# Cross attention and a leaky-ReLU layer on one core: tokens loaded a batch earlier, a gate ahead of their casts, another order in batches 3 to 6

## Chip, core and metric

The kernel runs on one core of one Trainium2 chip. The metric is the device time of one execution in microseconds. Three runs of the kernel before took 202.87 to 203.16 us, with a median of 203.11.

## What is computed

There are 8 batches. Each has 8 heads with 512 tokens and 32 state rows of 64 numbers. Tokens read the state and the state reads the tokens, both with a softmax. The results are laid side by side (544 rows of 512 numbers a batch) and go through a two-layer network.

```python
scores = scale * np.matmul(x, state.transpose(0, 1, 3, 2))
a = softmax(scores)                     # minus the maximum, exp, over (sum + 1e-9)
xread = np.matmul(a, state)
scores2 = scale * np.matmul(state, x.transpose(0, 1, 3, 2))
a2 = softmax(scores2)
sread = np.matmul(a2, x)
attn = np.concatenate([xread, sread], axis=2)
...
h = x @ w_in                            # x: attn as (8 * 544, 512); w_in 512 x 2048
g = np.maximum(0.01 * h, h)
return (g @ w_out).astype(np.float32)   # w_out 2048 x 512
```

## The kernel before

The token rows of a batch go through the first layer without `xread` being formed: the state is multiplied by `w_in` once per batch (the tile `M`, in four column blocks `c`), and `h` is the product of the probabilities `aT` with `M`. The second layer of a batch is a Strassen-like scheme: seven products `n` = 1 to 7 of eight steps each, with sums of halves of `hT` (`su0` to `su3`) and sums of the weights (`tw_...`). One step is a *unit*: two matmuls of 256 columns. A quarter of the first layer (`FastQuad`) is done with seven products too, with sums `lq`.

The work is software-pipelined over batches. While batch `b` has its first layer, batch `b - 1` finishes its second layer, batch `b + 1` has its scores and softmax, and the tokens of batch `b + 2` are loaded (one fp32 buffer `xl`), cast to bf16 by GpSimd (`xb`) and transposed by DMA (`xT`).

Every engine works through its own instructions in the order in which the code issues them; semaphores tie the engines together. SyncE (SP) issues the DMAs of that list in order too. In batches 3 to 6 the order is a string, `ORDER`, which `stretch` goes through token by token. Batches 0 to 2 and 7 are written out. Only the order within each engine counts. The tokens:

- `u`: the next unit, of the batch before while it has any, then of this batch (15 of 56 are done in a batch's own stretch). `d.n`, `dn.n`: what follows product `n`: a copy out of PSUM (1, 6, 5, 7) or a join with a saved copy into the output tile (2, 3, 4), and behind 3 and 4 the output's DMA. `sb.n.m`, `sn.n.m`: four steps (m to m+3) of the sum `su n`, for the batch before or this one.
- `f.j`, `r.j`: block `j` of the first layer (two matmuls of 512 columns into a PSUM tile `ph`, of which there are two) and its leaky ReLU on ScalarE, L411.
- `qs.i`, `g.n`, `gt.n`, `gl`, `gr`: the quad's sums `lq` (L635, two instructions each), products (two matmuls of 256 columns, tile `pl`, L651), evictions and joins (L663 on ScalarE or VectorE, join L666), the GpSimd addition and the ReLUs.
- `S`, `tp`, `rw`, `ls`, `x2`, `ex`, `e2`, `rc`, `ml`, `p2`: the next batch's scores (tile `sc`), first maxima (`mrow`, L226), their transpose (`mrowb`, L234), the subtraction (`sh`, L239), second maxima, exponentials, sums and reciprocals, products, second reciprocals.
- `mk.c`, `ev.c.g`: block `c` of `M` on TensorE and its eviction, whole (`g` = 2) or by halves, on ScalarE (`A`) or VectorE (`V`). A `3` belongs to this batch, the others to the next.
- `loads`, `casts.h`, `turn`: the load of tokens, the cast of two heads, the DMA transpose `xT`. `a2t`: the DMA transpose of the second probabilities. `rows`: in odd batches the state's reads of two batches (`psn`, 64 small matmuls) and their scaling `sr_n`. `rows_t`: their DMA transpose in batch 4. `late.i`: a sum of weights in batch `i`.

Some tiles share buffers by a tag. The quad's saved copies lie where `mrowb` (`gt.1`) and `sh` (`gt.5`) were, and its sums `lq` share two buffers with `xT`.

Of the kernel before, what the change touches and what calls it, by code (L numbers as in the profile page):

```python
# [9 lines left out]
P = 128  # L10
B, H, S, D = 8, 8, 512, 64
NS = 32
DFF = 2048
DM = 512
# [9 lines left out]
FP32 = mybir.dt.float32  # L24
# [6 lines left out]
def kernel(  # L31
# [9 lines left out]
    nc = tc.nc  # L41

    consts = ctx.enter_context(tc.tile_pool(name="consts", bufs=1))
# [61 lines left out]
    def load_x(b, eng):  # L105
        xl[b] = xpool.tile([P, H, NT * D], FP32, name="xl", tag="xl", bufs=1)
        eng.dma_start(xl[b][:], x[b].rearrange("h (p t) d -> p h (t d)", t=NT))

    def open_xb(b):
        xs[b] = xpool.tile([P, NT, H, D], BF16, name="xb", tag="xb")  # L110
# [88 lines left out]
    def a_xt_dma(a):  # L199
        nc.sync.dma_start_transpose(  # L200
            a.xT[:].rearrange("p t k q -> p (t k) q"),
            a.xb[:].rearrange("p t h d -> p (t h d)"),
        )
# [223 lines left out]
    class FastIn:  # L427
# [62 lines left out]
        def done(self, r, n, bank):  # L490
            R = self.R
            if n == 1:
                pool, tag, bufs, n4 = ((xpool, "xb", 4, 2), (mpool, "M", 2, 4))[r]
                ts = [pool.tile([P, n4, R * P], FP32, name=f"sf{r}", tag=tag, bufs=bufs) for _ in range(4 // n4)]
                self.sv[r] = dict(zip((1, 6, 5, 7), [t[:, i] for t in ts for i in range(n4)]))
            sv = self.sv[r]
            flat = bank.rearrange("p q t -> p (q t)")

            def relu(i, c, src):
                nc.scalar.activation(  # L500
                    out=self.hT[:, 8 * i + R * r:8 * i + R * (r + 1), P * c:P * (c + 1)],
                    in_=src.rearrange("p (q t) -> p q t", q=R), func=AF.Prelu, alpha=0.01,
                )

            if n in (1, 6, 7):
                SCA(sv[n], flat)
            elif n == 5:
                VEC(sv[n], flat)
            if n in (2, 3):
                k = {2: 1, 3: 6}[n]  # L510
                nc.vector.tensor_tensor(out=sv[k], in0=flat, in1=sv[k], op=ALU.add)
                relu(0, n - 2, sv[k])
            elif n == 7:
                nc.gpsimd.tensor_tensor(out=sv[5], in0=sv[7], in1=sv[5], op=ALU.add)
            elif n == 4:
                relu(1, 1, sv[5])
                relu(1, 0, flat)
# [192 lines left out]
    HC = DM // 2  # L710
# [68 lines left out]
    class Batch:  # L779
# [44 lines left out]
        def done(self, n, bank, copy=SCA):  # L824
            f = self.f
            if n in (1, 6, 5, 7):
                f.save(n, bank, copy)
            if n == 2:
                f.join(self.yo(0)[:, :, :HC], bank, 1)
                if self.b == B - 1:  # L830
                    self.out(0, slice(0, HC))
            elif n == 7:
                nc.gpsimd.tensor_tensor(  # L833
                    out=self.yo(1)[:, :, HC:], in0=f.sv[7][:], in1=f.sv[5][:], op=ALU.add
                )
                if self.b == B - 1:
                    self.out(1, slice(HC, DM))
            elif n == 3:
                f.join(self.yo(0)[:, :, HC:], bank, 6)
                self.out(0, slice(HC if self.b == B - 1 else 0, DM))  # L840
            elif n == 4:
                f.join(self.yo(1)[:, :, :HC], bank, 7)
                self.out(1)
# [355 lines left out]
        before.f.sums(n, 0, 4)  # L1199
    a_a2t(a1)  # L1200

    def stretch(b, hT, before, now, order):
        a, nxt = att_of[b], att_of[b + 1]
        rel, pm = {}, {}

        def u():
            (before if before.units else now).run(1, quiet=True)

        def f(j):
            rel[j] = ff1(a, hT, j, later=True)

        def mk(c, tag):
            pm[c] = a_m(a if c == 3 else nxt, c, tag)

        def ev(c, g, copy):
            t, src = (a if c == 3 else nxt), pm[c]
            if g == 2:
                copy(t.M[:, :, DM * c:DM * (c + 1)], src[:])  # L1220
            else:
                copy(t.M[:, g, DM * c:DM * (c + 1)], src[g][:] if isinstance(src, list) else src[:, g, :])

        def rows():
            if b % 2:
                a_sread_rows([att_of[b - 2], att_of[b - 1]])

        def loads():
            if b + 2 < B:
                load_x(b + 2, nc.sync)  # L1230

        def casts(h):
            if b + 2 < B:
                if h == 0:
                    open_xb(b + 2)
                cast_x(b + 2, h, h + 2, POO)

        def turn():
            if b + 2 < B:
                a_open(att_of[b + 2], b + 2)  # L1240
                a_xt_dma(att_of[b + 2])

        def rows_t():
            if b == 4:
                sread_t(0, 3)

        def late(i):
            if b == i:
                fi.w_sum(2 * (b - (B - 3)))

        def qs(i):
            if i == 0:
                fq_of[b] = FastQuad(a, 8)
                fq_of[b].hT = hT
            fq_of[b].sums(i)

        table = dict(
            u=u, f=f, r=lambda j: rel.pop(j)(), S=lambda: a_scores(nxt), mk=mk, ev=ev, rows=rows, loads=loads,
            casts=casts, turn=turn, late=late, rows_t=rows_t,
            tp=lambda: a_top(nxt), rw=lambda: a_rows(nxt), ls=lambda: a_less(nxt), x2=lambda: a_max2(nxt),  # L1260
            ex=lambda: a_exp(nxt), e2=lambda g: a_exp2(nxt, g), rc=lambda: a_probs(nxt, 0), ml=lambda: a_probs(nxt, 1),
            p2=lambda: a_probs2(nxt), a2t=lambda: a_a2t(a),
            sb=lambda n, m, k=4: before.f.sums(n, m, m + k), sn=lambda n, m: now.f.sums(n, m, m + 4),
            d=lambda n, copy=SCA: before.done(n, before.bank[n], copy), dn=lambda n, copy=SCA: now.done(n, now.bank[n], copy),
            g=lambda n: fq_of[b].product(n), gt=lambda n, copy=None: fq_of[b].take(n, copy),
            gl=lambda: fq_of[b].last(), gr=lambda i, c: fq_of[b].relu(i, c), qs=qs,
        )
        for name in order.split():
            name, *args = name.split(".")
            table[name](*(int(v) if v.isdigit() else {"A": SCA, "V": VEC}.get(v, v) for v in args))  # L1270

    fi = FastIn(None)
    fq_of = {}
    ORDER = (
# [8 lines left out]
    )  # L1283

    for b in range(2, B):
        hT = hpool.tile([P, 16, S], BF16, name="hT", tag="hT")
        a = att_of[b]
        nxt = att_of[b + 1] if b + 1 < B else None
# [17 lines left out]
        for s in range(16):  # L1306
# [68 lines left out]
            if s == (9 if b == 2 else 7) and b + 2 < B:  # L1375
                a_open(att_of[b + 2], b + 2)
                a_xt_dma(att_of[b + 2])
            if nxt is not None:
                if b == 2 and s < ms:
                    if s in (8, 9):  # L1380
                        a_exp2(nxt, s - 8)
                    elif s == 7:
                        a_exp(nxt)
                        weights_sum(3, 0, 4)
                        a_probs(nxt, 0)
                elif s == 5:
                    a_exp(nxt)
                elif s in (7, 8):
                    a_exp2(nxt, s - 7)
                    if s == 7:  # L1390
                        a_probs(nxt)
                elif s == ms + 1:
                    for some in ((a1, a2, nxt) if b == 2 else (nxt,)):
                        a_probs2(some)
                elif s in (ms + 2, ms + 3):
                    SCA(nxt.M[:, s - ms - 2, DM:2 * DM], pm1[:, s - ms - 2, :])
# [36 lines left out]
    u, v = [psum.tile([P, 1, HC], FP32, name="yu", tag="ph")[:] for _ in range(2)]  # L1433
# [65 lines left out]
```

## Time and profile before

| | |
|---|---|
| median of three runs | 203.11 us (202.87 to 203.16) |
| profiled execution | 202.62 us, of which the span from the first to the last instruction is 200.8 |
| TensorE (PE) busy | 193.4 us, 96% of the span |
| VectorE (DVE) busy | 169.1 us, 84% |
| ScalarE (ACT) busy | 148.3 us, 74% |
| GpSimd (POOL) busy | 61.5 us, 31% |
| moved by DMA | 28.02 MB, mean 139 GB/s |

Times in the views are microseconds from the span's start. A line of the timeline gives start, duration, engine, line of the code, operation, output and inputs, shapes and a count; in brackets stands the idle time ahead of it and what ended it. A matmul's duration includes its way through the array, so matmuls that follow each other without a gap overlap: their starts tell the pace. A group's line gives count, busy time and the mean duration in nanoseconds. Some matmul records are missing in the trace (three in each of these batches).

### The profile page before, as it was taken

How to read it: one execution, taken by the hardware profiler on the slowest of the kernel's cores; microseconds unless marked ns; L12 is line 12 of the kernel's file. 1: busy time of each engine (PE TensorE's matmuls, PEld its weight loads, DVE VectorE, ACT ScalarE, POOL GpSimd, SP SyncE). 2: the span in 40 equal slices, each digit the busy share in tenths (PEclk: the TensorE clock that was granted, in tenths of full speed). 3: DMA queues.
4: the chain of work that ended last, by engine and by line, in shares of the span. 5: the costliest groups of instructions: out<-in, count | busy, mean ns of one | idle time of the engine just before them, and what ended most of it. 6: DMA issues, size and time to landing. Idle time of an engine off the chain costs nothing.

```text
span 200.8 us, 5078 instructions
## 1 busy us (share of the span) xinstructions
PE 193.4 (96%) x2068; PEld 137.1 (68%) x2090; DVE 169.1 (84%) x285; ACT 148.3 (74%) x275; POOL 61.5 (31%) x86
## 2 busy tenths in 40 slices
PE   7999999999999999899999999999999999999992
PEld 2666634346676766776776677677767788799882
DVE  2576689998999999998999799999999977995622
ACT  3378848499877858797899778987898768767710
POOL 8392175790047004220413040400040024004250
PEclk9999999999999999999999999999999999999999
DMA  6999997999661960539162935161006502210035
GB/s 199 215 206 266 236 295 139 226 277 203 139 193 30 302 210 9 108 141 268 64 124 102 265 111 106 69 172 25 3 37 207 99 0 90 122 55 0 5 91 170
DMA packets 39511, 28.02 MB, mean 139 GB/s; under 512 B 25344, under 2 KB 36736, under 8 KB 39488
## 3 DMA queue, kind: packets, MB, share of 16 engines
q1 hardware_dynamic: 33712, 20.35, 38.6%
q0 software_dynamic: 4944, 6.55, 16.1%
q10 hardware_dynamic: 832, 0.79, 1.2%
q8 instruction: 16, 0.26, 0.5%
q14 instruction: 7, 0.06, 0.1%
HBM read 17.30 MB, written 8.91 MB: 131 GB/s over the span
## 4 chain that ended last, share of the span: by engine, by line
PE 76%; DVE 16%; ACT 2%; DMA 2%; issue 2%; DVEq 0%
PE yq L761 32%; PE ph L405 12%; PE py L690 4%; PE pyw L690 3%; PE pf L483 3%; PE yu L761 3%; PE ph L1040 3%; PE pm L384 3%; DVE su L750 3%; DVE lq L635 2%; PE pspin L142 2%; PE pl L651 2%; DMA a2T<-e 2%; PE pl L572 2%; DVE yo L773 2%
## 5 line engine op out<-in xcount | busy, mean ns | idle before, releaser
L411 ACT ACTIVATE hT<-ph 128x512 bf16<-128x512 f32 x84 | 49.0, 605 | 13.3 <-PE ph L405 6.6
L761 PEld LDWEIGHTS <-su 128*128 128x128 bf16 x480 | 45.9, 98 | 13.8 <-issue 0.8
L405 PE MATMUL ph<-aT,M 128*128 128x512 bf16 x148 | 43.5, 379 | 0.4
L761 PEld LDWEIGHTS <-hT 128*128 128x128 bf16 x336 | 32.3, 98 | 12.6 <-issue 2.5
L761 PE MATMUL yq<-tw_xf,su 128*128 128x256 bf16 x224 | 32.8, 273 | 0.2
L761 PE MATMUL yq<-w_out_bf,hT 128*128 128x256 bf16 x224 | 30.3, 273 | 0.3
L113 POOL CAST xb<-xl 128x512 bf16<-128x512 f32 (+1 forms) x24 | 13.6, 608 | 47.5 <-DMA xl<-in_x_dram 36.9
L833 POOL TENSOR_TENSOR yo<-sv,sv 128x512 f32<-128x512 f32 x7 | 9.1, 1298 | 37.5 <-ACT hT L411 28.1
L405 PEld LDWEIGHTS <-M 128*128 128x128 bf16 x168 | 16.4, 98 | 6.2 <-DVE tw_x L727 0.2
L750 DVE TENSOR_TENSOR su<-hT 128x1024 bf16<-128x1024 bf16 (+1 forms) x27 | 18.8, 702 | 0.8 <-ACT hT L411 0.6
L770 ACT COPY sv<-yq 128x512 f32<-128x512 f32 x24 | 13.9, 585 | 5.5 <-PE yq L761 5.4
L761 PE MATMUL yq<-tw_x,su 128*128 128x256 bf16 x112 | 16.1, 273 | 0.0
L761 PE MATMUL yq<-w_out_bf,su 128*128 128x256 bf16 x112 | 16.0, 273 | 0.1
L773 DVE TENSOR_TENSOR yo<-yq,sv 128x512 f32<-128x512 f32 x20 | 13.5, 675 | 1.8 <-PE yq L761 1.5
L761 PE MATMUL yq<-tw_x,hT 128*128 128x256 bf16 x104 | 13.9, 273 | 0.0
L304 ACT ACTIVATE e<-sc,mcol 128x512 bf16<-128x512 f32 x16 | 11.0, 694 | 0.1
L663 ACT COPY ls<-pl 128x512 f32<-128x512 f32 x16 | 9.0, 587 | 2.4 <-PE pl L651 2.3
L690 PEld LDWEIGHTS <-hT 128*128 128x128 bf16 x64 | 5.9, 98 | 7.0 <-issue 1.1
L750 DVE TENSOR_TENSOR su<-su,hT 128x1024 bf16<-128x1024 bf16 x14 | 9.6, 686 | 0.2
L298 DVE TENSOR_REDUCE mcol<-sc 128x2 f32<-128x1024 f32 x8 | 9.7, 1214 | 0.0
L226 DVE TRANSPOSE_TENSOR_REDUCE mrow<-sc 128x32 f32<-128x1024 f32 x7 | 8.7, 1244 | 0.9 <-PE sc L216 0.9
L750 DVE TENSOR_TENSOR su<-hT,su 128x2048 bf16<-128x2048 bf16 (+1 forms) x8 | 9.3, 1157 | 0.0
(193 smaller groups left out, 361.8 us busy)
## 6 DMA issues: line engine op xcount, KB each, us to landing
out_dram<-yo SPq DMA_DIRECT2D x12, 512.0 KB, 3.2
xl<-in_x_dram SPq DMA_DIRECT2D x5, 1024.0 KB, 6.0
w_in_bf<-in_moe_w_in_dram POOLq DMA_DIRECT2D x4, 512.0 KB, 7.8
w_out_bf<-in_moe_w_out_dram POOLq DMA_DIRECT2D x2, 512.0 KB, 12.3
x<-in_x_dram POOLq DMA_DIRECT2D x2, 512.0 KB, 11.2
w_out_bf<-in_moe_w_out_dram POOLq DMA_DIRECT2D x4, 256.0 KB, 13.5
xl<-in_x_dram POOLq DMA_DIRECT2D x1, 1024.0 KB, 17.2
out_dram<-ysb SPq DMA_DIRECT2D x4, 256.0 KB, 5.8
```

Source lines behind the costliest of these rows:

```text
L113: copy(xs[b][:, :, h0:h1].rearrange("p t h d -> p h t d"), xl[b][:, h0:h1].rearrange("p h (t d) -> p h t d", t=NT),)
L298: nc.vector.tensor_reduce(out=a.m2[:], in_=a.sc[:], axis=AX.X, op=ALU.max, negate=True)
L304: nc.scalar.activation(out=a.e2[:, g], in_=a.sc[:, g, :], func=AF.Exp, bias=a.m2[:, g:g + 1], accum_out=a.r2[:, g:g + 1],)
L405: nc.tensor.matmul(ph[:], lhsT=a.M[:, g, P * j:P * (j + 1)], rhs=a.aT[:, g, :], start=(g == 0), stop=(g == 1),)
L411: nc.scalar.activation(out=hT[:, j, :], in_=ph[:], func=AF.Prelu, scale=1.0 / SCALE, alpha=0.01)
L663: copy(self.sv[n], flat)
L690: nc.tensor.matmul(y.py, lhsT=hT[:, j, P * i:P * (i + 1)], rhs=w_out_bf[:, j, :], start=(j == 0), stop=(j == 15),)
L750: (eng or nc.vector).tensor_tensor(out=S[n][:, ms], in0=u[:, ms], in1=v[:, ms], op=op)
L761: nc.tensor.matmul(bank[:, i, :], lhsT=lhs[:, m, P * i:P * (i + 1)], rhs=rhs[:, m, :], start=(first and m == 0 and (i == 0 or of is not No ...
L770: copy(t[:], bank)
L773: nc.vector.tensor_tensor(out=dst, in0=bank, in1=self.sv[n][:], op=ALU.add)
L833: nc.gpsimd.tensor_tensor(out=self.yo(1)[:, :, HC:], in0=f.sv[7][:], in1=f.sv[5][:], op=ALU.add)
```

## The change

- **Loads.** `loads` fetches the tokens of batch `b + 3` instead of `b + 2`, and the token stands behind `turn` instead of near the head of the list. Batch 2 issues one load more, for batch 5, behind its transpose.
- **Gate.** A new token `gate`: GpSimd copies one column of the first maxima into a small tile `after`. It stands behind `tp` and ahead of the casts in GpSimd's order, so the casts start when the first maxima of this stretch are done.
- **Outputs.** The output half behind product 3 goes in two transfers of 256 KB instead of one of 512 KB, in batches 2, 3 and 4.
- **Order.** `ORDER` is a new list with the same tokens, but for the gate, `ev.3` in two halves instead of one, and `ev.0.0` on ScalarE instead of VectorE. Among the moves: `f.0` behind `S` and `mk.3`, `qs.1` ahead of `ls`, `sb.2.4` behind `gt.2`, `a2t` from the end to behind `qs.2`, `g.5` ahead of `g.6` and `g.4` ahead of `g.3`, `p2` and `rows_t` to the end.

```diff
             elif n == 3:
                 f.join(self.yo(0)[:, :, HC:], bank, 6)
-                self.out(0, slice(HC if self.b == B - 1 else 0, DM))
+                for i in range(2) if self.b in (2, 3, 4) else (None,):
+                    self.out(0, slice(HC if self.b == B - 1 else 0, DM), i)
...
         def loads():
+            if b + 3 < B:
+                load_x(b + 3, nc.sync)
+
+        def gate():
             if b + 2 < B:
-                load_x(b + 2, nc.sync)
+                nc.gpsimd.tensor_copy(after[:], nxt.m1[:, :1])
...
-            casts=casts, turn=turn, late=late, rows_t=rows_t,
+            casts=casts, gate=gate, turn=turn, late=late, rows_t=rows_t,
...
+    after = consts.tile([P, 1], FP32, name="after")
...
     ORDER = (
-        "sb.0.4 f.0 u qs.0 loads sb.1.4 rows S mk.3.big r.0 u f.1 casts.0 u casts.2 u casts.4 tp "
-        "u r.1 ev.3.2.A d.2 rw ls u f.3 u u u casts.6 f.2 u g.1 qs.1 qs.2 turn u sb.2.4 qs.3 u "
-        "g.2 d.6.A r.2 r.3 gt.1.A u gt.2.V sb.3.0.8 x2 u u f.5 f.4 u r.5 u ex d.5.A u u f.6 u u "
-        "g.6 u g.5 u u u u u u rows_t d.7.V r.4 gt.6.A gt.5.A g.7 r.6 gt.7.A u f.7 e2.0 r.7 gl "
-        "f.12 u u u g.3 rc e2.1 g.4 u r.12 u u u gt.3.V u d.3 u late.5 mk.2.ph gr.1.0 gr.0.1 "
-        "ev.2.0.A gr.1.1 mk.1.sc mk.0.big late.6 ev.2.1.A gr.0.0 ml u u u d.4 sn.0.0 u f.13 r.13 "
-        "u u f.14 u u p2 u u f.15 u r.14 ev.1.2.A r.15 u u u u ev.0.0.V sn.1.0 sn.2.0 u u u "
-        "ev.0.1.A dn.1 a2t "
+        "sb.0.4 qs.0 u sb.1.4 rows S mk.3.big f.0 u u u u u f.1 f.3 u tp gate u u f.2 d.2 r.0 r.1 "
+        "casts.0 casts.2 casts.4 casts.6 ev.3.0.A ev.3.1.A rw u u qs.1 ls u u u u g.1 g.2 u r.2 "
+        "qs.2 a2t turn loads qs.3 d.6.A u r.3 u u gt.1.A u gt.2.V sb.2.4 sb.3.0.8 x2 f.5 f.4 ex "
+        "g.5 g.6 u u u f.6 r.5 d.5.A r.4 gt.6.A r.6 gt.5.A u f.12 u u u u u g.7 e2.0 gt.7.A f.7 u "
+        "u r.12 r.7 e2.1 d.7.V rc g.4 gl g.3 u u u u gt.3.V late.5 gr.1.0 d.3 u u u ml mk.2.ph "
+        "gr.0.1 late.6 ev.2.0.A ev.2.1.A mk.0.big gr.0.0 gr.1.1 mk.1.sc u u u f.13 d.4 sn.0.0 u "
+        "ev.0.0.A f.14 u sn.1.0 u u r.13 u u u f.15 r.14 ev.1.2.A u u u u u r.15 u ev.0.1.A u u "
+        "dn.1 sn.2.0 p2 rows_t "
     )
...
             if s == (9 if b == 2 else 7) and b + 2 < B:
                 a_open(att_of[b + 2], b + 2)
                 a_xt_dma(att_of[b + 2])
+                load_x(b + 3, nc.sync)
```

## The prediction, made before the result was known

> **What bounds the kernel now.** I read the busy shares first, then the four repeated stretches of the middle, then TensorE's order of time in them, and last what its few gaps wait for.
>
> ```profile
> span 200.8 us, 5078 instructions
> ...
> PE 193.4 (96%) x2068; PEld 137.1 (68%) x2090; DVE 169.1 (84%) x285; ACT 148.3 (74%) x275; POOL 61.5 (31%) x86
> ```
>
> TensorE (PE) is busy 96% of the span. The change works in batches 3 to 6, so I cut the trace where a unit's PE order begins anew in each of them: at 70.74, 92.74, 113.41, 134.71 and 155.19 us. The view of windows gives, per stretch: its length, then the busy time of PE, of weight loads, of VectorE (DVE), ScalarE (ACT) and GpSimd (POOL), the clock and the DMA share.
>
> ```profile
> 70.74:92.74 22.00, 21.12 (x254) 15.48 (x254) 21.39 (x37) 17.70 (x33) 4.96 (x6) 1.00 0.48 133
> 92.74:113.41 20.67, 20.49 (x190) 14.91 (x191) 19.74 (x35) 17.75 (x33) 4.89 (x6) 1.00 0.53 139
> 113.41:134.71 21.30, 21.09 (x254) 15.50 (x255) 19.89 (x35) 17.75 (x33) 4.77 (x6) 1.00 0.47 135
> 134.71:155.19 20.48, 20.32 (x189) 14.89 (x190) 19.78 (x36) 17.86 (x33) 2.50 (x2) 1.00 0.24 65
> ```
>
> The same work takes 22.00, 20.67, 21.30 and 20.48 us. Batches 3 and 5 also hold the 64 small matmuls of `psn` (token `rows`). The clock is 1.00 throughout, so the differences are waits. VectorE is nearly full too, most of all in batch 3. The timeline of PE has the waits:
>
> ```profile
> 71.48 0.70 PE L350 MATMUL psn<-xb,a2T 128*32 128x64 bf16 x64
> 72.11 0.41 PE L216 MATMUL sc<-xT,st_t 64*32 64x512 bf16 x8
> ...
> 79.64 0.60 PE L761 MATMUL yq<-tw_x,su 128*128 128x256 bf16 x4
> 80.96 0.38 PE L651 MATMUL pl<-lq 128*128 128x256 bf16 x2 [0.72 <-DVE ls L666]
> ...
> 101.01 0.60 PE L761 MATMUL yq<-tw_x,su 128*128 128x256 bf16 x4
> 101.63 0.38 PE L651 MATMUL pl<-lq 128*128 128x256 bf16 x2
> ...
> 114.15 0.88 PE L350 MATMUL psn<-xb,a2T 128*32 128x64 bf16 x64
> 114.96 0.41 PE L216 MATMUL sc<-xT,st_t 64*32 64x512 bf16 x8
> ...
> 134.71 0.59 PE L405 MATMUL ph<-aT,M 128*128 128x512 bf16 x2
> 135.14 0.38 PE L761 MATMUL yq<-w_out_bf,hT 128*128 128x256 bf16 x2
> ```
>
> The last pair is the price list: an `f` (two matmuls of 512 columns) takes PE 0.43, so one of 256 columns 0.109 and a unit `u` (two of them) 0.22. Hence the four matmuls of 79.64 are through at 80.08, and the quad's product starts at 80.96: 0.88 lost. In batch 4 it is 101.45 to 101.63: 0.18. In batch 6 there is no such gap. `psn` takes 0.63 in batch 3 and 0.81 in batch 5: 0.18 more. Together 1.24 us, and this fits the windows: 20.48 of batch 6 as the floor, 21.11 with `psn`, so (22.00 - 21.11) + (20.67 - 20.48) + (21.30 - 21.11) = 1.27. More than that the stretches cannot give while PE's work stays, and the change leaves its matmuls as they are (56 units, 12 `f`, 7 products in either list).
>
> **The cause of the gaps.** The product that waits is the first after `gt.2`, VectorE's join at L666; it may not write its PSUM tile before that join has read the tile. VectorE is late because of what stands ahead of the join:
>
> ```profile
> 76.75 0.70 DVE L635 TENSOR_TENSOR lq<-M 128x256 bf16<-128x256 bf16 x1
> ...
> 78.60 0.69 DVE L635 TENSOR_TENSOR lq<-aT,lq 128x256 bf16<-128x256 bf16 x1
> 79.22 0.68 DVE L750 TENSOR_TENSOR su<-hT 128x1024 bf16<-128x1024 bf16 x1
> ...
> 80.22 0.68 DVE L666 TENSOR_TENSOR ls<-pl,ls 128x512 f32<-128x512 f32 x1
> ...
> 136.12 1.24 DVE L226 TRANSPOSE_TENSOR_REDUCE mrow<-sc 128x32 f32<-128x1024 f32 x1
> ...
> 137.87 1.23 DVE L234 STREAM_TRANSPOSE mrowb<-mrow 128x1024 f32<-128x1024 f32 x1
> 139.19 1.23 DVE L239 TENSOR_TENSOR sh<-sc,mrowb 128x1024 f32<-128x1024 f32 x1
> 140.34 0.28 DVE L635 TENSOR_TENSOR lq<-M 128x256 bf16<-128x256 bf16 x1
> ...
> 141.14 0.69 DVE L750 TENSOR_TENSOR su<-hT 128x1024 bf16<-128x1024 bf16 x1
> ...
> 142.15 0.68 DVE L666 TENSOR_TENSOR ls<-pl,ls 128x512 f32<-128x512 f32 x1
> ```
>
> Four sums `lq` take 76.75 to 79.22 = 2.47 in batch 3 and 140.34 to 141.14 = 0.80 in batch 6: 0.42 more each. What differs is POOL:
>
> ```profile
> 76.69 2.46 POOL L113 CAST xb<-xl 128x512 bf16<-128x512 f32 x4 [12.83 <-DMA xl<-in_x_dram]
> ...
> 97.23 2.40 POOL L113 CAST xb<-xl 128x512 bf16<-128x512 f32 x4 [10.82 <-DMA xl<-in_x_dram]
> ...
> 117.80 2.28 POOL L113 CAST xb<-xl 128x512 bf16<-128x512 f32 x4 [10.63 <-issue]
> ```
>
> The casts start when the load lands and lie on all four sums in batch 3, on some in batch 4, hardly on them in batch 5; batch 6 has none. There they lie on the first maxima's transposes and on the subtraction from PSUM, which keep their 1.23.
>
> The Trainium skill (SBUF — State Buffer, Who interferes with whom) says that a VectorE instruction with two SBUF inputs and a POOL instruction that reads SBUF exclude each other, the loser blocked for the whole instruction. By that a sum met by a cast waits up to one whole cast, 0.6 us; the trace's 0.42 on top of 0.20 is the milder price. With 0.6 for two sums, 1.2 instead of 0.84, the slack reckoned below would be 0.4 us smaller.
>
> **Tokens a batch ahead, casts behind the gate.** The load moves from the stretch's head to behind the turn of the stretch before.
>
> ```profile
> xl<-in_x_dram SPq DMA_DIRECT2D x5, 1024.0 KB, 6.0
> ...
> 63.93 1.80 SPq L200 DMA_TRANSPOSE xT<-xb  x1
> 65.83 2.21 SPq L800 DMA_DIRECT2D out_dram<-yo  x2
> 68.13 0.41 SPq L107 DMA_DIRECT2D xl<-in_x_dram  x1
> ```
>
> A load lands 6.0 us after its issue, 8.6 at worst (68.13 to 76.69, beside two output transfers). Issued behind the casts and the 1.8 us of `turn`'s transposes, some 7 us into a stretch, it is there 5 us or more before the next stretch's gate. Only batch 3's is near: it follows the transposes of 63.93, so 65.8 + 8.6 = 74.4 against a gate near 73.8 (scores at 72.11, 0.41 for them and 1.24 for the maxima); its casts may start 0.6 late. No wait of SP for the casts costs anything: behind it are only the load and outputs due 7 us later.
>
> The gate is a one-element copy per partition (a few tenths on an idle POOL; nothing but casts stands behind it) that waits for the first maxima. In batch 6 those end at 136.12 + 1.24 - 134.71 = 2.65 after the stretch's start, in the new order up to 0.4 earlier; so the casts run from about 2.6 to 5.0, over the join `d.2`, the transpose `rw` and `qs.1`. The first two I price at nothing, as in batch 5; the two sums of `qs.1` cost 0 to 0.84 extra, and I take 0.7.
>
> **New order on VectorE.** In batch 6, where nothing disturbs, `gt.2` ends at 142.83, 8.12 after the start. The new list puts `sb.2.4` behind it (0.60, 141.14 to 141.74) and fills the bubble between `rw` and `ls` with `qs.1` (137.87 + 1.23 - 139.19: at most 0.1 to 0.17), in all -0.7: 7.4 without casts, 8.1 with my 0.7. The product `g.5` now stands one `f` and one unit earlier: old 101.45 - 92.74 = 8.71, new 8.06. So with casts it would be even, with nothing else changed. But the scores come one `f` earlier on PE (0.43), and VectorE reaches the first maxima up to 0.4 earlier: slack -0.05 to 0.35 in batch 4, 0.3 more in batches 3 and 5 (`psn` holds PE 0.63, VectorE's `sr_n` about half of that), 0.7 or more in batch 6. I take a wait of 0.05 in batch 4, none elsewhere. `sb.2.4`, now behind the join, is due one unit and two products later (0.65) and takes 0.6: the same slack.
>
> **New order on ScalarE.** `ev.0.0` comes over from VectorE, and `ev.3` is split: about 0.6 us more for ACT.
>
> ```profile
> 106.99 0.60 ACT L674 ACTIVATE hT<-pl 128x512 bf16<-128x512 f32 x1
> ...
> 109.99 1.16 ACT L411 ACTIVATE hT<-ph 128x512 bf16<-128x512 f32 x2
> ```
> ```profile
> L304 ACT ACTIVATE e<-sc,mcol 128x512 bf16<-128x512 f32 x16 | 11.0, 694 | 0.1
> L1220 ACT CAST M<-pm 128x1024 bf16<-128x1024 f32 x8 | 8.1, 1007 | 0.0
> L246 ACT ACTIVATE e<-sh 128x1024 bf16<-128x1024 f32 x7 | 7.4, 1054 | 0.4 <-DVE sh L239 0.4
> ```
>
> Six evictions of 128x512 from 106.99 to 109.99 are 0.50 each. From the end of `ls` (whose buffer `gt.1` needs) to the end of `r.15` the new list has 19 of these, one `ex`, two `e2`, one `ev.1.2` and `r.15`: 9.5 + 1.05 + 1.4 + 1.0 + 0.6 = 13.55. In batch 6 `ls` ends 5.71 after the start (139.19 + 1.23); with `qs.1` ahead of it (0.40 - 0.1), 0.7 for the casts and up to 0.4 less at the head it is 6.3 to 6.7. So `r.15` ends at 19.85 to 20.25 of 20.48, before the `u` that opens the next stretch needs it. `r.13` ends 2.1 earlier, at 17.75 to 18.15; `f.15`, which takes its PSUM slot, stands eight units and itself before the end, at 18.3. `g.4` comes 1.09 behind `g.7` (an `f`, two `u`, a product), and `gt.7` between them takes some 1.0. No stall by this sum; I allow 0.05 in all.
>
> **Transposed exponentials earlier.** `a2t` moves from the stretch's end to its middle.
>
> ```profile
> 110.23 1.45 SPq L323 DMA_TRANSPOSE a2T<-e  x1
> ```
>
> Issued at 110.23, it kept `psn` of batch 5 waiting at 114.15. Its input is a stretch old, so in the new place it issues as soon as SP has sent the outputs before it. The 0.18 goes; next late there is nothing but PE's own order.
>
> **Outputs in two transfers.**
>
> ```profile
> out_dram<-yo SPq DMA_DIRECT2D x12, 512.0 KB, 3.2
> ```
>
> An output half lands 3.2 us after issue and its buffer is rewritten by the next `d.2`, 8 us later. One issue more on SP, with nothing urgent behind: 0, at most 0.1. `p2` and `rows_t` at the end: 0, since VectorE has an idle us there.
>
> **Sum.** -(0.88 + 0.18 + 0.18) + 0.05 + 0.05 = -1.14 us on a span of 200.8 (profiled time 202.62, so 1.8 lie outside the span). The median of the three runs is 203.11, 0.49 above the profiled run; the difference carries over: 203.11 - 1.14 = 201.97, so 201.95.
>
> **The rivals.** (1) *The subtraction `ls` becomes the late step: slower.* It now stands behind `qs.1` under the casts, and both `gt.1` (buffer of `mrowb`), hence `gt.2` and `g.5`, and ACT's 13.55 us hang on it. From an `ls` that ends 6.9 us after the start, instead of 6.3, `r.13` and `r.15` come after their readers: some 0.5 per stretch, in four stretches 2.0, so 203.11 - 1.24 + 2.0 = 203.9. For it: ACT is 17.75 of 20.67 already and has a longer list. Against: only batch 4 has casts without `psn`'s 0.63.
> (2) *The wait is only moved:* `g.5` waits 0.2 to 0.25 for `gt.2` in batches 3, 4 and 5: -1.24 + 0.7 = -0.54, 202.55.
> (3) *The change doesn't reach batch 3:* the load issued at 65.8 lands so late that the casts still lie on the later sums. It needs 76 us or more, a landing in over 10 us, more than any here. Then 0.88 stays, and with it the gain is 0.3: 202.8.
> (4) *More:* VectorE enters batch 7 some tenths earlier and PE's small gaps there shrink: 201.6.
>
> **How the numbers follow.** Forecast 0.56 (201.7 to 202.2), more 0.08, moved wait 0.15, no reach 0.06, slower 0.15. About 0.2% (0.4 us) is what a measurement of this kernel can tell from no change: below 202.7 is faster. Forecast, more and most of the moved wait are faster: 0.75; the rest of it and (3) are the same: 0.10; (1): 0.15. The range takes in (4) with 0.2 of noise and (2) and (3), and leaves out most of (1): 201.35 to 203.1.
>
> **What would show it.** Right: the stretches take about 21.1, 20.5, 21.1 and 20.5; casts start within 0.5 us of the first maxima's end; only two `lq` of each stretch take over 0.5; `psn` 0.63 in batches 3 and 5. Wrong: PE gaps before `pl<-lq`, before the `ph` of `f.15` or at a stretch's first `u`, or ScalarE without idle time and PE waiting for L411.

## The result: 201.68 us, 0.3 to 0.6% faster, and the profile after

The changed kernel took 201.68 us in the median of six runs (201.17 to 202.16), the kernel before 202.99 in six runs (202.48 to 203.41). The ratio is 0.9938, with a 95% interval of 0.9916 to 0.9959. The profiled execution took 201.17 us; it is the fastest of the six. A later series gave less: 201.62 us in twelve runs against 202.39 in 31 of the kernel before, ratio 0.9966 (0.9949 to 0.9984). The two intervals overlap, so the gain is 0.3 to 0.6%. From the page of the changed kernel:

```profile
span 199.4 us, 5110 instructions
...
PE 194.0 (97%) x2090; PEld 136.2 (68%) x2090; DVE 165.5 (83%) x281; ACT 149.7 (75%) x283; POOL 61.7 (31%) x89
```

The view of windows, cut where a stretch's PE order begins (now with the first `u`); the columns are those of before:

```profile
70.88:91.99 21.11, 21.11 (x256) 15.48 (x254) 18.71 (x34) 18.01 (x35) 4.90 (x7) 1.00 0.81 221
91.99:112.47 20.48, 20.48 (x193) 14.94 (x191) 18.88 (x33) 18.12 (x35) 4.97 (x7) 1.00 0.51 136
112.47:133.57 21.10, 21.10 (x256) 15.49 (x254) 20.53 (x35) 18.12 (x35) 4.98 (x7) 1.00 0.35 91
133.57:154.05 20.48, 20.48 (x193) 14.94 (x191) 19.56 (x36) 18.12 (x35) 2.51 (x2) 1.00 0.18 61
```

PE is busy in all of each stretch. Their sum falls from 84.45 to 83.17 us: 1.28 of the 1.45 between the two profiled executions (202.62 and 201.17). The rest lies outside them, 0.14 later at the head and 0.31 shorter behind batch 6, where the change moves next to nothing; I did not find its cause. The timeline of PE shows the three places that had waits:

```profile
71.20 0.70 PE L350 MATMUL psn<-xb,a2T 128*32 128x64 bf16 x64
71.83 0.41 PE L216 MATMUL sc<-xT,st_t 64*32 64x512 bf16 x8
...
78.71 1.03 PE L405 MATMUL ph<-aT,M 128*128 128x512 bf16 x4
79.57 0.60 PE L651 MATMUL pl<-lq 128*128 128x256 bf16 x4
...
99.18 1.03 PE L405 MATMUL ph<-aT,M 128*128 128x512 bf16 x4
100.05 0.60 PE L651 MATMUL pl<-lq 128*128 128x256 bf16 x4
...
112.78 0.70 PE L350 MATMUL psn<-xb,a2T 128*32 128x64 bf16 x64
113.41 0.41 PE L216 MATMUL sc<-xT,st_t 64*32 64x512 bf16 x8
```

Four matmuls of 512 columns need 4 x 0.216 = 0.86, so the quad's products at 79.57 and 100.05 follow without a gap, and `psn` takes 0.63 in both odd batches. VectorE in batch 4, and POOL in batches 3 and 5:

```profile
95.97 0.48 DVE L635 TENSOR_TENSOR lq<-M 128x256 bf16<-128x256 bf16 x1
96.38 0.69 DVE L635 TENSOR_TENSOR lq<-aT 128x256 bf16<-128x256 bf16 x1
...
98.13 0.28 DVE L635 TENSOR_TENSOR lq<-lq,M 128x256 bf16<-128x256 bf16 x1
...
98.95 0.69 DVE L666 TENSOR_TENSOR ls<-pl,ls 128x512 f32<-128x512 f32 x1
```
```profile
73.87 0.19 POOL L1233 COPY after<-mrow 128x1 f32<-128x1 f32 x1 [9.92 <-DVE mrow L226]
74.00 2.28 POOL L113 CAST xb<-xl 128x512 bf16<-128x512 f32 x4
...
115.28 0.19 POOL L1233 COPY after<-mrow 128x1 f32<-128x1 f32 x1 [9.21 <-DVE mrow L226]
115.41 2.35 POOL L113 CAST xb<-xl 128x512 bf16<-128x512 f32 x4
```

The casts follow the gate at once; two sums still meet them (0.48 and 0.69 against 0.28) and those behind `ls` no longer. The join ends at 98.95 + 0.69 = 99.64, 0.4 before its product. One line was not foreseen. It is the join `d.2` of batch 3, which writes the output tile that batch 1 used. With it stand the two SP issues in front of it, and the landing times of batch 1's two outputs by the view of the tile `yo`, first of the changed kernel, then of the kernel before:

```profile
74.74 0.69 DVE L773 TENSOR_TENSOR yo<-yq,sv 128x512 f32<-128x512 f32 x1 [0.93 <-DMA out_dram<-yo]
```
```profile
65.91 1.08 SPq L107 DMA_DIRECT2D xl<-in_x_dram  x1
67.09 1.10 SPq L800 DMA_DIRECT2D out_dram<-yo  x2
```
```profile
DMA to landing us min/median/max: 7.6/8.3/9.0
```
```profile
DMA to landing us min/median/max: 3.6/3.9/4.2
```

The load that batch 2 now issues stands right ahead of two outputs, and they land in 7.6 to 9.0 us instead of 3.6 to 4.2. VectorE waits 0.93 us for the buffer. In this execution PE did not notice.

### The profile page after: what moved, and what is told of

It is laid out like the page before. It is cut to its first block, busy times and chain, and to the rows that moved or that the text cites. A ratio compares the mean times of both kernels' runs of the same rounds, so it can differ in the third digit from the quotient of the medians.

```text
span 199.4 us, 5110 instructions
## 1 busy us (share of the span) xinstructions
PE 194.0 (97%) x2090; PEld 136.2 (68%) x2090; DVE 165.5 (83%) x281; ACT 149.7 (75%) x283; POOL 61.7 (31%) x89
## 4 chain that ended last, share of the span: by engine, by line
PE 79%; DMA 16%; POOL 3%; issue 0%; DVE 0%; POOLq 0%
PE yq L761 43%; PE ph L405 18%; DMA xl<-in_x_dram 9%; DMA w_in_bf<-in_moe_w_in_dram 5%; PE pf L483 3%; PE yu L761 3%; PE pl L651 3%; PE pm L384 3%; DMA xT<-xb 2%; PE pl L572 2%; PE psn L350 1%; PE sc L216 1%; PE py L690 1%; PE phw L418 1%; POOL w_in_bf L126 1%; POOL xb L113 1%
## 5 line engine op out<-in xcount | busy, mean ns | idle before, releaser
L405 PE MATMUL ph<-aT,M 128*128 128x512 bf16 x168 | 47.6, 379 | 0.0
L761 PE MATMUL yq<-tw_xf,su 128*128 128x256 bf16 x224 | 30.8, 273 | 0.0
L761 PE MATMUL yq<-w_out_bf,hT 128*128 128x256 bf16 x224 | 29.0, 273 | 0.0
L761 PE MATMUL yq<-w_out_bf,su 128*128 128x256 bf16 x112 | 15.3, 273 | 0.0
L1221 ACT CAST M<-pm 128x512 bf16<-128x512 f32 x24 | 13.5, 597 | 0.0
L663 ACT COPY ls<-pl 128x512 f32<-128x512 f32 x16 | 9.5, 594 | 1.8 <-PE pl L651 1.1
```

Of the source, the lines that this page charges most:

```text
L405: nc.tensor.matmul(ph[:], lhsT=a.M[:, g, P * j:P * (j + 1)], rhs=a.aT[:, g, :], start=(g == 0), stop=(g == 1),)
L663: copy(self.sv[n], flat)
L761: nc.tensor.matmul(bank[:, i, :], lhsT=lhs[:, m, P * i:P * (i + 1)], rhs=rhs[:, m, :], start=(first and m == 0 and (i == 0 or of is not No ...
```

## Experiments

My theory was that the waits before came from casts lying on the sums ahead of the join, and that the new place of loads and casts, the new order and the earlier `a2t` each take a share. The main rival was that the order alone does it. Ratios are to the kernel before, run on the same chip in the same series, with 95% intervals; PE gaps are read from the starts of its matmuls. The diffs are cuts: of `ORDER` they show the tokens that move, and what stands behind a `#` is a note.

### Loads and gate in the old order

Beside the moved tokens, `loads`, `gate` and batch 2's extra load are those of the change.

```diff
-"... qs.0 loads sb.1.4 ..." "... casts.0 u casts.2 u casts.4 tp ..." "... qs.2 turn u ..."
+"... qs.0 sb.1.4 ..." "... u u tp gate casts.0 casts.2 casts.4 ..." "... qs.2 turn loads u ..."
```

> The kernel before with its old order; only the loads a batch earlier and the casts behind the gate. If the casts over the quad's sums made the waits for the join L666 (my theory), the four sums ahead of it take about 0.8 us in every batch, the waits of 0.88 in batch 3 and 0.18 in batch 4 go, and the 0.18 of psn in batch 5 stays: stretches of about 21.1, 20.5, 21.3 and 20.5, 1.05 us faster than before. If the order is what matters (rival), about half of the 0.88 stays and the time is within 0.5 us of before.

201.97 us (201.46 to 203.25), ratio 0.9994 (0.9972 to 1.0016): no difference from before. VectorE and PE of batch 3:

```profile
75.11 0.69 DVE L773 TENSOR_TENSOR yo<-yq,sv 128x512 f32<-128x512 f32 x1 [1.53 <-DMA out_dram<-yo]
...
78.13 0.28 DVE L635 TENSOR_TENSOR lq<-M 128x256 bf16<-128x256 bf16 x1
...
78.73 0.28 DVE L635 TENSOR_TENSOR lq<-aT,lq 128x256 bf16<-128x256 bf16 x1
```
```profile
75.86 0.38 PE L761 MATMUL yq<-tw_xf,su 128*128 128x256 bf16 x2 [0.24 <-DVE yo L773]
...
80.68 0.38 PE L651 MATMUL pl<-lq 128*128 128x256 bf16 x2 [0.21 <-DVE ls L666]
```

All four sums are back at 0.28, as expected. But the join's wait for its buffer is 1.53 here, and PE loses 0.40 at the first unit behind it, 0.37 at the quad's product and 0.11 between: 0.88, as much as before. The time expected was missed: one wait went and another of the same size came. The time is the one that the rival gave, but not for its reason.

### The same with batch 2's load sooner

The extra load goes right behind the casts that free its buffer, ahead of two DMA transposes and the outputs in SP's order.

```diff
                     for h in range(0, H, 2):
                         cast_x(b + 2, h, h + 2, POO)
+                    if b == 2:
+                        load_x(5, nc.sync)
...
-                load_x(b + 3, nc.sync)      # behind a_xt_dma of batch 2
```

> The old order with loads a batch earlier and the gate, as in the first experiment, but with batch 2's load issued near 60.5 us. There, the sums were no longer slow (all under 0.4 us), yet PE lost 0.88 in batch 3 as before, by a join that waited 1.5 us for the output's buffer. If the casts were the cause before and the outputs behind the load took the gain back (theory): no wait of the join, no PE gap in batch 3 or 4, about 0.18 left at psn of batch 5, 1.0 us faster than before. Rival: the old order has no slack of its own; 0.3 or more stays in batch 3.

201.59 us (201.18 to 201.80), ratio 0.9954 (0.9939 to 0.9969). VectorE and PE of batch 3:

```profile
73.36 0.65 DVE L773 TENSOR_TENSOR yo<-yq,sv 128x512 f32<-128x512 f32 x1
...
76.34 0.28 DVE L635 TENSOR_TENSOR lq<-M 128x256 bf16<-128x256 bf16 x1
...
78.15 0.68 DVE L666 TENSOR_TENSOR ls<-pl,ls 128x512 f32<-128x512 f32 x1
```
```profile
79.22 0.60 PE L761 MATMUL yq<-tw_x,su 128*128 128x256 bf16 x4
79.66 0.38 PE L651 MATMUL pl<-lq 128*128 128x256 bf16 x2
```

No wait of the join, no slow sum, no PE gap; only `psn` of batch 5 keeps its 0.18. So the casts were the cause of the waits before, moving them suffices in the old order too, and in the first experiment it was the load ahead of the outputs that took the gain back.

### The new order alone

```diff
-"sb.0.4 qs.0 u ..." "... tp gate u u ..." "... a2t turn loads qs.3 ..."
+"sb.0.4 qs.0 loads u ..." "... tp u u ..." "... a2t turn qs.3 ..."      # loads: b + 2, as before
```

> The changed kernel with the loads where they were (a batch's tokens fetched at the stretch's head) and no gate. My theory: the casts start when the load lands, 5 to 6 us after the start, and lie on the subtraction and on the sums behind it; in batch 3 three or four sums at 0.6 instead of 0.2, join L666 1.2 to 1.7 us later than in the changed kernel, PE waits 0.7 to 1.2 there and up to 0.4 in batches 4 and 5: 0.2 to 1.0 us slower than the changed kernel. Rival: the order with sb.2.4 behind the join has enough slack alone, no wait over 0.1, time equal to the changed kernel.

201.55 us (200.98 to 201.86), ratio 0.9954 (0.9939 to 0.9970). VectorE and PE of batch 3:

```profile
76.91 0.70 DVE L635 TENSOR_TENSOR lq<-aT,lq 128x256 bf16<-128x256 bf16 x1
...
78.15 0.69 DVE L635 TENSOR_TENSOR lq<-lq,aT 128x256 bf16<-128x256 bf16 x1
78.76 0.68 DVE L666 TENSOR_TENSOR ls<-pl,ls 128x512 f32<-128x512 f32 x1
```
```profile
78.46 1.03 PE L405 MATMUL ph<-aT,M 128*128 128x512 bf16 x4
79.49 0.60 PE L651 MATMUL pl<-lq 128*128 128x256 bf16 x4
```

Three sums are slow (1.2 us together), yet the join is only 0.17 late, and there is no gap in batches 4 and 5. I had expected a wait of 0.7 to 1.2: the rival was nearer. This kernel keeps the split outputs and the moved evictions of the change. Its order is worth about as much as moving the casts, and the two do not add up to twice that. The changed kernel was not run in this series; its two ratios, 0.9938 and 0.9966, lie on either side of 0.9954, so no gain of the moved loads on top of the order is shown.

### One token of the order

```diff
-"... turn u sb.2.4 qs.3 u ..." "... gt.2.V sb.3.0.8 ..."
+"... turn u qs.3 u ..." "... gt.2.V sb.2.4 sb.3.0.8 ..."
```

> The kernel before with a single token moved: sb.2.4 behind the join gt.2. Theory: the join ends 0.60 earlier, with the casts on the sums as before; the PE gap of batch 3 goes from 0.88 to 0.28, that of batch 4 from 0.18 to 0; 0.78 us faster, if the moved sum isn't missed by its units (due 0.2 us behind the product in the old order: then some of it comes back there). Rival: the gap stays, as the join waits for something else: equal to before.

202.17 us (201.51 to 202.58), ratio 0.9984 (0.9966 to 1.0002). PE of batch 3, and at `psn` of batch 5:

```profile
80.73 0.39 PE L761 MATMUL yq<-tw_x,su 128*128 128x256 bf16 x2 [0.23 <-DVE su L750]
...
114.54 0.42 PE L350 MATMUL psn<-xb,a2T 128*32 128x64 bf16 x32 [0.52 <-DMA a2T<-e]
```

The wait before the product of batch 3 shrank from 0.88 to 0.21, and 0.39 came back at the unit that needs the moved sum: 0.60 in all. Batch 4's gap is gone. But `psn` of batch 5, 0.54 earlier than in the kernel before, waits longer for `a2T`: it takes 1.28 (113.61 to 114.89), 0.65 above its 0.63, where the kernel before lost 0.18. The three losses make 1.25 against 1.24 before, so this execution, the slowest of its twelve, gains nothing; the median's 0.30 is not clear of no change. Moved by itself, the sum is late for its own units; the rest of the new list (`f.5 f.4` ahead of the product, more units before that sum) makes room for it.

### The gate

Without it (`gate` struck from the list), and with it one step later (a copy of a column of `rw`'s result; `gate` and the casts stand behind `rw`):

```diff
-"... u tp gate u u ..."
+"... u tp u u ..."
```
```diff
-nc.gpsimd.tensor_copy(after[:], nxt.m1[:, :1])
+nc.gpsimd.tensor_copy(after[:], nxt.mb[:, 0, :1])
...
-"... u tp gate u u ..." "casts.0 casts.2 casts.4 casts.6 ev.3.0.A ev.3.1.A rw u u ..."
+"... u tp u u ..." "ev.3.0.A ev.3.1.A rw gate casts.0 casts.2 casts.4 casts.6 u u ..."
```

> The changed kernel without the gate. The tokens are there a batch early, so the casts of batches 4 and 5 start as soon as GpSimd and the buffer are free, at or before the stretch's head, over sb.0.4, qs.0 and sb.1.4 or over the sums before. If the gate matters (theory): those sums of 1024 take 0.9 to 1.3 instead of 0.68, the first maxima come 0.5 to 1 us later and PE waits some tenths in batches 4 and 5, 0.2 to 0.8 us slower than the changed kernel. Rival: VectorE has idle time at the head, and nothing is lost: equal within 0.1 in the PE stretches.

201.62 us (200.93 to 202.42), ratio 0.9963 (0.9944 to 0.9981). No gap in batches 4 and 5: batch 4's casts run at the end of the stretch before (from 86.48), batch 5's right behind `psn` (114.23), which reads the buffer that they write. The gaps are in batch 3 (0.70 behind `d.2`, which waits 2.0 us for the outputs, and 0.37 at the product), so this run did not judge the gate; the one on taking back, below, does.

> The changed kernel with the gate behind the transpose rw instead of the first maxima, so that the casts start about 1.5 to 2 us later and lie on qs.1, the subtraction, qs.2 and qs.3 on purpose. Theory: two to four sums at 0.6 more often, join L666 0.8 to 1.7 us later; as the changed kernel has about 0.3 to 0.7 us of slack at the product behind the join, PE waits 0.3 to 1.0 us in each of batches 3, 4 and 5: 1 to 2.5 us slower than the changed kernel. Rival (casts don't matter): no change.

202.66 us (200.94 to 203.28), ratio 0.9992 (0.9970 to 1.0015). PE of batch 3:

```profile
80.89 0.60 PE L651 MATMUL pl<-lq 128*128 128x256 bf16 x4 [1.03 <-DVE ls L666]
```

Batch 3 loses 0.48 behind `d.2` and 1.20 here. Batches 4 and 5 lose nothing, though two sums behind `ls` are slow in each (0.69): I had expected 0.3 to 1.0. In batch 4 the join still ends 0.2 before its product, in batch 5 0.05. In batch 3 two sums are slow too (0.67 and 0.69), behind a `d.2` that waits 1.80 for the outputs. The run without the gate has no slow sum there, and although its `d.2` waits longer, 2.0, its product loses only 0.37: the slow sums make the difference of 0.83. So the rival fails in batch 3; for 4 and 5 I had the slack too small.

### The load of batch 5 and the outputs

The changed kernel with batch 5's load at the head of batch 3, where it was before; with the load sooner, as in the second experiment; the same again; and beside that the changed kernel itself.

```diff
+        def first():                    # token behind qs.0
+            if b == 3:
+                load_x(5, nc.sync)
...
-                load_x(b + 3, nc.sync)  # batch 2
```

> The changed kernel without batch 2's extra load; batch 5's tokens are loaded at the head of batch 3 as in the kernel before, the other loads stay early. Theory: no wait of the join for its buffer in batch 3, casts there from about 76.3 us over the subtraction and three or four sums (0.6 each), a PE gap of 0.1 to 0.2 at the product behind the join; none in batches 4 to 6. Time within 0.3 us of the changed kernel.

201.46 us (201.21 to 201.97), ratio 0.9958 (0.9941 to 0.9974). No wait of `d.2`, four slow sums in batch 3, a gap of 0.47 at the product (0.1 to 0.2 expected).

> The changed kernel with batch 2's extra load issued right behind the casts that free its buffer (near 60.5 us), ahead of the transposes and the outputs on SP, instead of right ahead of the two outputs. Theory: in the changed kernel the outputs of batch 1 lie behind the load and land 8.3 us after issue instead of 3.9, so that the join d.2 of batch 3 waits 0.9 us for its buffer; on other executions that reaches PE. Here the outputs land in about 4 us, the join doesn't wait, PE has no gap, and qs.1 of batch 3 falls under the casts (two slow sums, as in batches 4 and 5). Time 0 to 0.5 us under the changed kernel, with less spread. Rival: the wait is covered by slack in every execution: equal time.

201.05 us (200.76 to 201.51), ratio 0.9937 (0.9914 to 0.9961). SP, and VectorE's join:

```profile
60.72 0.39 SPq L107 DMA_DIRECT2D xl<-in_x_dram  x1
...
67.11 1.01 SPq L800 DMA_DIRECT2D out_dram<-yo  x2
```
```profile
73.59 0.65 DVE L773 TENSOR_TENSOR yo<-yq,sv 128x512 f32<-128x512 f32 x1
```

The outputs land in 3.0 to 4.0 us, the join does not wait, and PE has no gap in batches 3 to 6. Against the old order with the same load (201.59, same series) that is 0.54 less, of which `psn` explains 0.18; the intervals overlap.

> The changed kernel itself, beside the other three: its profile shows the join's wait for the output's buffer in batch 3 again (0.5 to 2 us), with or without a PE gap behind it.

201.62 us (200.99 to 202.40), ratio 0.9966 (0.9949 to 0.9984). PE of batch 3:

```profile
79.86 0.60 PE L651 MATMUL pl<-lq 128*128 128x256 bf16 x4 [0.20 <-DVE ls L666]
```

Here `d.2` waited 1.47 us, and PE lost 0.15 behind it and 0.37 at this product. So the same kernel has executions with this loss (0.52) and without.

> The changed kernel with the sooner load once more, on the same chip as the changed kernel itself, to compare the two: 0 to 0.6 us under it, no wait of the join in batch 3.

200.97 us (200.65 to 202.19), ratio 0.9937 (0.9916 to 0.9957), no wait and no gap again. Against 201.62 of the changed kernel in the same series that is 0.65 less, about the 0.52 that its profile loses; the intervals of the two ratios overlap slightly. It has the lowest median of all kernels here.

### `a2t` at its old place

```diff
-"qs.2 a2t turn loads ..." "... sn.2.0 p2 rows_t "
+"qs.2 turn loads ..." "... sn.2.0 p2 rows_t a2t "
```

> The changed kernel with a2t back at the stretch's end. Theory: the transposed exponentials of batch 4 are issued only when SP comes to them near 110 us and land some 3.7 to 4.3 us later, while psn of batch 5 now comes near 112.8, about 1.4 us sooner than in the kernel before: PE waits 0.2 to 1.5 us at psn in batch 5, nowhere else. Rival: psn's longer time in batch 5 had another cause, and psn takes 0.63 here too: equal to the changed kernel.

202.77 us (202.22 to 203.26), ratio 1.0021 (1.0007 to 1.0036): slower than the kernel before. PE and SP around `psn` of batch 5:

```profile
112.63 0.42 PE L350 MATMUL psn<-xb,a2T 128*32 128x64 bf16 x32
113.94 0.42 PE L350 MATMUL psn<-xb,a2T 128*32 128x64 bf16 x32 [0.89 <-DMA a2T<-e]
114.29 0.41 PE L216 MATMUL sc<-xT,st_t 64*32 64x512 bf16 x8
```
```profile
109.08 1.34 SPq L365 DMA_TRANSPOSE sr_t<-sr_n  x1
110.52 1.26 SPq L323 DMA_TRANSPOSE a2T<-e  x1
```

`psn` takes 1.66 instead of 0.63, with PE waiting at its middle, where the second batch's exponentials begin. The new list brings `psn` forward and puts `rows_t` ahead of `a2t` on SP; without `a2t`'s move the change would have lost there what it won elsewhere. "Nowhere else" was missed: the product of batch 3 also waits, 0.23, behind a `d.2` that waited 1.19 for the outputs.

### Three parts taken back at once

The changed kernel with the sooner load, without the gate, with whole output halves, `ev.0.0` on VectorE and `ev.3` in one.

```diff
-"... tp gate u u ..." "... ev.3.0.A ev.3.1.A ..." "... ev.0.0.A ..."
+"... tp u u ..." "... ev.3.2.A ..." "... ev.0.0.V ..."
...
-                for i in range(2) if self.b in (2, 3, 4) else (None,):
-                    self.out(0, slice(HC if self.b == B - 1 else 0, DM), i)
+                self.out(0, slice(HC if self.b == B - 1 else 0, DM))
```

> The changed kernel with batch 2's load near 60.5 us, and three parts of the change taken back at once: no gate, whole output halves, ev.0.0 on VectorE and ev.3 in one piece. Theory: none of the three carries time; VectorE gets 0.67 us more per stretch of some 1 to 2 it has idle; no PE gap over 0.1 in batches 3 to 6, equal to the kernel with the sooner load alone. Rival: the gate is what keeps the casts off (the first no-gate run lost time only through the late outputs, so this is open): sums of 1024 slowed at the stretches' ends, PE gaps of 0.2 to 0.6 in batches 4 and 5.

201.31 us (200.99 to 202.13), ratio 0.9958 (0.9942 to 0.9974). No PE gap in batches 3 to 6 and no slow sum, so none of the three carries time there. Its median is 0.3 above the kernel with the sooner load alone, and the intervals overlap. The profiled execution (202.05, the second slowest of twelve) loses 0.8 of PE in batch 7:

```profile
189.62 1.03 PE L761 MATMUL yu<-tw_xf,su 128*128 128x256 bf16 x8 [0.63 <-DVE yhs L773]
```

VectorE is late there by a sum that took 1.79 instead of 0.69 (last section). Whether that is the whole difference of the medians stays open.

## Why the prediction held, step by step

**The sum of the waits** was right in the first profile: 1.24 forecast, 1.28 gone, and the stretches are 21.11, 20.48, 21.10 and 20.48 as written. In the second, 0.52 came back in batch 3, 0.37 of it as a gap before `pl<-lq`, which I had named as a sign of being wrong; 1.24 less 0.52 is 0.72. Forecast 201.95, measured 201.68, against a median before of 202.99 instead of 203.11. The forecast gain of 1.14 lies between the 1.31 of the first series and the 0.77 of the second; that it came so near the first is in part luck, as one loss was left out. The +0.05 each for batch 4 and ScalarE were not needed: the join of batch 4 ends 0.4 before its product (forecast -0.05 to 0.35), and ScalarE's `r.15` there ends at 111.91, 19.92 after the stretch's start (forecast 19.85 to 20.25).

**Casts and sums.** In batches 4 and 5 two sums of `qs.1` are slow, 0.20 and 0.41 extra: 0.6 together against 0.7. In batch 3 there are none, for a reason that I did not have: `d.2` was held, and `qs.1` came behind the casts.

**Outputs** is the step that was wrong. I had "its buffer is rewritten by the next `d.2`, 8 us later" and 0 to 0.1, for the one issue more; I gave no price to batch 2's load ahead of the outputs. In batch 3 it is rewritten 6.7 us after the issue, near 73.8, and the outputs land late because the load stands before them. I had reckoned what outputs do to a load (8.6 us), and forgot what a load does to the outputs behind it. It cost 0.93 of VectorE in one profile, covered, and 0.52 of PE in the other. That second case is rival (2), a moved wait, by a step that it did not name and in one batch instead of three.

**What carries the gain** was half right. The casts were the cause, and the new order needs `a2t`'s move (`psn` loses 1.03 without it). But I treated the moved casts and the new order as shares of one sum, "even" in batch 4 with casts. Each brings much of it without the other: ratio 0.9954 by the order with the old loads, and 0.9954 by loads and gate in the old order, once batch 2's load is issued sooner. With that load where the change has it, loads and gate alone brought nothing (0.9994). The gate, the split outputs and the move of `ev.0.0`, taken back together, left no gap. Of the rivals, a late `ls` did not stall ScalarE's readers: in the second profile it ended 7.8 after batch 3's start, 7.1 without `psn`'s 0.63 and later than rival (1)'s 6.9, and no `ph` or first `u` waited. The load of batch 2 was in time: its casts began with the gate at 74.00.

## What to carry to other kernels

A DMA moved ahead in a queue must be priced for what is queued behind it, with the buffers that those transfers free, and not for its own landing alone. Where one wait has two remedies, try each alone: the second may add only slack, and the profile of one execution can hide a wait that another shows. An operation that is free at its place, as `a2t` before, may become the late one when its reader is moved forward.

## What the runs showed of the hardware

A 256-column sum on VectorE that meets a running cast on POOL takes up to 0.70 us instead of 0.28. For longer sums both outcomes are on record, and they go with which of the two instructions began first. In batch 7 a sum of 1024 columns with two inputs falls together with an addition on POOL. The first pair of lines is from the last experiment (three parts taken back), the second from the repeat of the changed kernel with the sooner load:

```profile
187.45 1.79 DVE L750 TENSOR_TENSOR su<-hs,su 128x1024 bf16<-128x1024 bf16 x1
...
187.42 1.27 POOL L833 TENSOR_TENSOR yo<-sv,sv 128x512 f32<-128x512 f32 x1 [3.36 <-issue]
```
```profile
186.99 0.69 DVE L750 TENSOR_TENSOR su<-hs,su 128x1024 bf16<-128x1024 bf16 x1
...
187.33 1.47 POOL L833 TENSOR_TENSOR yo<-sv,sv 128x512 f32<-128x512 f32 x1 [3.36 <-issue]
```

Where the addition began 0.03 ahead, it kept its 1.27 and the sum took 1.10 more than its 0.69. Where the sum began 0.34 ahead, it kept its 0.69 and the addition took 0.20 more. In all other profiles of this document the sum is ahead too; why it was late in this one execution is not known. In the last experiment four casts also took 2.79 (from 85.31) instead of 2.28, with the product `aT` (1024 columns, two inputs) on VectorE at 86.39, which kept its 0.69.
